# Value transforms that read strided columns of the loaded v, and query casts moved between the Sinkhorn steps

## The chip, the core and the metric

The kernel runs on one core of a Trainium2 chip. The core has a matrix engine (TensorE, PE in the profile; its weight loads are listed as PEld), a vector engine (VectorE, DVE), a scalar engine (ScalarE, ACT), a general engine (GpSimd, POOL) and a queue that only issues transfers (SyncE, SP). Engines run their own instruction streams in order and wait for one another through semaphores. The metric is the device time of one execution in microseconds; lower is better.

## The reference, cut to what matters

The inputs are q, k and v of 4 batches x 8 heads x 768 tokens x 64 (f32), a matrix sort_net of 8 x 8 for every batch and head, and the weights of a two-layer network.

```
P = sort_net                                   # [4, 8, 8, 8]
for _ in range(5):
    P = exp(P - max(P, -1)); P /= sum(P, -1) + 1e-9; P /= sum(P, -2) + 1e-9
k_sorted = einsum('bhij,bhjcd->bhicd', P, k_blocks)   # 8 blocks of 96 tokens
v_sorted = einsum('bhij,bhjcd->bhicd', P, v_blocks)
attn     = softmax(q_blocks @ k_sorted^T / 8)         # inside each block
x        = attn @ v_sorted, laid out as [3072, 512]
out      = (s * relu(x @ w_in)^2 + b) @ w_out         # [3072,512] -> 2048 -> 512
```

So each of the 8 blocks of k and v is first replaced by a mix of the 8 blocks, with the weights P that the five Sinkhorn rounds give; then follow attention inside each block and a large feed-forward network.

## The kernel before, in words

**The mix as a matmul.** A batch of k or v is loaded as a tile of 128 partitions: 8 heads x 8 blocks x 2 halves of a block. A partition holds 48 tokens (c) x 64 features (d). One column of that tile, as TensorE weights against a block-diagonal matrix built from P (`PD[b]`, in `build_pd`, L199), gives the mixed values. For k (and, with a fixed selection matrix `qid`, for q) `qk_piece` (L227) takes the 64 features of one token c as weights, `src[:, c0 + c, :]`, which lie side by side. For v, `v_piece` (L244) needs the 48 tokens of one feature d as weights, padded with zeros to 64 (`GAP`). In the loaded tile these lie 64 elements apart. The kernel before therefore makes a permuted copy `VP` (d outer, c inner), and `v_piece` reads `VP[b % 2][:, d0 + d, :]`, 64 neighbouring elements. A piece is 16 features x 2 halves, so 32 matmuls with 64 columns of weights and 64 moving columns, and one evacuation from PSUM by ScalarE ("A") or VectorE ("D"). Four pieces make a batch of v, three a batch of k or q.

**Where the copy of v comes from.** For batch 0, v is loaded as f32 by SP's queue in four parts (`v0f`, L75 to L79), and ScalarE casts and permutes a part (`permute`, L152) after each of the exps 2 to 5 of the Sinkhorn loop (L176 to L195). For batches 1 to 3, a POOL-issued load casts v to bf16 into `rawv` (`load`, L83), and POOL itself permutes it in eight copies (`v_sort`, L449, called at L453 and L514).

**The order at the start.** The program is written out by hand; each engine executes in the order of the text. PE first runs 30 matmuls on zeros (`warm`, L146 and L175), then the three query pieces, the matmul in `build_pd(0)`, 3 more on zeros, and then v, v, k, k, k, v, v (L409 to L419), and then scores (`s_piece`), attention times values (`p_piece`) and transposes (`t_piece`) of batch 0. PSUM tiles with the tag "a" have three buffers, so a piece waits until the piece three before it has been evacuated. The first two query pieces are evacuated by ScalarE after the Sinkhorn loop, the third by VectorE after the block weights. POOL issues the loads of q and k in three parts each, makes the identity, `qid` and `emat`, and then issues the loads of w_in and w_out (`load_w`); eight such loads may be under way, the next waits for the oldest.

**The steady part.** For each batch `ffn1` (L348) and `ffn2` (L376) run over two halves of the tokens; the pieces of the next batch are set between the matmul groups of `ffn2` (`halves`, L487): k at slot 0, v pieces 0 to 2 at slot 8, the fourth v piece in the second half.

Of the kernel before, what the change touches and what calls it, by code (L numbers as in the profile page):

```python
# [9 lines left out]
FP = mybir.dt.float32  # L10
BF = mybir.dt.bfloat16
AF = mybir.ActivationFunctionType
ALU = mybir.AluOpType
AX = mybir.AxisListType


def spread(t, dims):

    return bass.AP(tensor=t.tensor, offset=t.offset, ap=[list(t.ap[0])] + dims)
# [3 lines left out]
def kernel(  # L23
# [12 lines left out]
    nc = tc.nc  # L36

    B, H, S, D = q.shape
    NB = sort_net.shape[-1]
    BLK = S // NB  # L40
    BH = B * H
# [6 lines left out]
    C2 = BLK // 2  # L48
    GAP = 64
# [3 lines left out]
    CK = 16  # L53
# [3 lines left out]
    raw = [t.rearrange("b h (j z c) d -> b (h j z) (c d)", j=NB, z=2) for t in (q, k, v)]  # L57

    const = ctx.enter_context(tc.tile_pool(name="const", bufs=1))
    rawp = ctx.enter_context(tc.tile_pool(name="rawp", bufs=2))  # L60
# [5 lines left out]
    gtp = ctx.enter_context(tc.tile_pool(name="gtp", bufs=2))  # L66
# [5 lines left out]

    sn = const.tile([BH, NB, NB], FP)
    nc.sync.dma_start(out=sn, in_=sort_net.rearrange("b h i j -> (b h) i j"))
    v0f = gtp.tile([128, C2, D], FP, tag="gt", name="v0f")  # L75
    CV = C2 // 4
    for c in range(0, C2, CV):
        nc.sync.dma_start(out=v0f[:, c:c + CV, :].rearrange("p c d -> p (c d)"),  # L78
                          in_=raw[2][0][:, c * D:(c + CV) * D])  # L79

    RAW = {}

    def load(t, b, parts=1):  # L83
        ti = rawp.tile([128, C2, D], BF, tag=f"raw{t}", name=f"raw{t}")
        RAW[t, b] = ti
        n = C2 // parts
        for c in range(0, C2, n):
            nc.gpsimd.dma_start(out=ti[:, c:c + n, :].rearrange("p c d -> p (c d)"),
                                in_=raw["qkv".index(t)][b][:, c * D:(c + n) * D])
# [11 lines left out]

    zeros = const.tile([128, 512], BF)
    nc.vector.memset(zeros, 0.0)  # L103
    VP = [const.tile([128, D, GAP], BF, name=f"vp{i}") for i in range(2)]
    KS = [const.tile([128, NG, 2, GAP], BF, name=f"ks{i}") for i in range(2)]
    VS = [const.tile([KR, 2 * NG, VW], BF, name=f"vs{i}") for i in range(2)]
    nc.vector.memset(VP[0][:, :, C2:GAP], 0.0)
    nc.vector.memset(KS[0][:, :, :, C2:GAP], 0.0)
    eps = const.tile([BH, NB], FP)
    nc.vector.memset(eps, 1e-9)  # L110

    load("q", 0, 3)
    load("k", 0, 3)


    ident = const.tile([128, 128], BF)
# [12 lines left out]
    def load_w():  # L129
        wiv = moe_w_in.rearrange("(a p) f -> p a f", p=128)  # L130
        for c in range(2):
            cs = slice(c * (d_ff // 2), (c + 1) * (d_ff // 2))
            for a in range(NHP):
                nc.gpsimd.dma_start(out=wi[:, a, cs], in_=wiv[:, a, cs])
        fill_vs(0)
        wov = moe_w_out.rearrange("(f p) n -> p f n", p=128)
        for c in range(4):
            fs = slice(c * (NF // 4), (c + 1) * (NF // 4))
            nc.gpsimd.dma_start(out=wo[:, fs, :], in_=wov[:, fs, :])
# [9 lines left out]
            nc.tensor.matmul(out=z, lhsT=zeros[:, 0:128], rhs=zeros, start=True, stop=True)  # L149


    def permute(eng, b, src, cs=slice(0, C2), ds=slice(0, D)):  # L152
        o = VP[b % 2][:, ds, cs]
        i = src[:, cs, ds].rearrange("p c d -> p d c")
        if eng is nc.scalar:
            eng.copy(out=o, in_=i)  # L156
        else:
            eng.tensor_copy(out=o, in_=i)  # L158


    rstat = const.tile([BH, NB], FP)
    rrec = const.tile([BH, NB], FP)
    jsel = const.tile([128, NB], FP)
# [9 lines left out]
    nc.vector.tensor_tensor(out=sn, in0=sn, in1=rstat.broadcast_to([BH, NB, NB]),  # L173
                            op=ALU.subtract)
    warm(30)  # L175
    for it in range(5):  # L176
        nc.scalar.activation(out=sn, in_=sn, func=AF.Exp)
        if it >= 1:
            permute(nc.scalar, 0, v0f, slice((it - 1) * CV, it * CV))
        if it == 2:  # L180
            load_w()
        if it in (1, 2):
            idle[it - 1]()
        nc.vector.tensor_reduce(out=rstat, in_=sn, axis=AX.X, op=ALU.add)
        nc.vector.reciprocal(out=rrec, in_=rstat)
        nc.vector.tensor_tensor(out=sn, in0=sn, in1=rrec.broadcast_to([BH, NB, NB]), op=ALU.mult)
        if it == 4:
            break
        nc.vector.tensor_reduce(out=rstat, in_=sn.rearrange("p i j -> p j i"),
                                axis=AX.X, op=ALU.add)  # L190
        if it == 0:
            nc.vector.tensor_tensor(out=rstat, in0=rstat, in1=eps, op=ALU.add)
        nc.vector.reciprocal(out=rrec, in_=rstat)
        nc.vector.tensor_tensor(out=sn, in0=sn, in1=spread(rrec, [[0, NB], list(rrec.ap[1])]),
                                op=ALU.mult)  # L195

    PD = {}

    def build_pd(b):  # L199
        pe = psb.tile([128, 512], FP, tag="b", name="pe")  # L200
        nc.tensor.matmul(out=pe[:, 0:NB * NB], lhsT=emat[:, b, :],
                         rhs=sn.rearrange("p i j -> p (i j)"), start=True, stop=True)
        tmp = rtp.tile([128, NB, NB], FP, tag="tmp", name="tmp")
        nc.vector.tensor_tensor(out=tmp, in0=pe[:, 0:NB * NB].rearrange("p (i j) -> p i j", j=NB),
                                in1=spread(jsel, [[0, NB], list(jsel.ap[1])]), op=ALU.mult)
        pt = rtp.tile([128, NB], FP, tag="pt", name="pt")
        nc.vector.tensor_reduce(out=pt, in_=tmp, axis=AX.X, op=ALU.add)
        cs = rtp.tile([128, 1], FP, tag="cs", name="cs")
        nc.vector.tensor_reduce(out=cs, in_=pt, axis=AX.X, op=ALU.add)
        rc = rtp.tile([128, 1], FP, tag="rc", name="rc")  # L210
        nc.vector.reciprocal(out=rc, in_=cs)
        pd = const.tile([128, 2, 2, NG], BF, name=f"pd{b}")
        nc.vector.scalar_tensor_tensor(
            out=pd.rearrange("p e z (a i) -> p (e z a) i", i=NB),
            in0=spread(bm, [list(bm.ap[1]), [0, NB]]), scalar=rc,
            in1=spread(pt, [[0, 4 * NHP], list(pt.ap[1])]), op0=ALU.mult, op1=ALU.mult)
        PD[b] = pd
# [9 lines left out]
    def qk_piece(t, b, c0, eng, first=None):  # L227
        if t == "q" and c0 == 0:
            QT[b] = trp.tile([128, NG, 2, C2], BF, tag="qt", name="qt")
        src = RAW[t, b]  # L230
        mov = qid.rearrange("p e z a j -> p e z (a j)") if t == "q" else PD[b]
        dst = QT[b] if t == "q" else KS[b % 2]
        ps = psa.tile([128, CK, 2, NG], FP, tag="a", name="tp")
        for c in range(CK):
            for e in range(2):
                nc.tensor.matmul(out=ps[e * 64:(e + 1) * 64, c].rearrange("p z g -> p (z g)"),  # L236
                                 lhsT=src[:, c0 + c, :],
                                 rhs=mov[:, e].rearrange("p z g -> p (z g)"),
                                 start=True, stop=True)
        if first is not None:  # L240
            first()
        evac(eng, dst[:, :, :, c0:c0 + CK], ps.rearrange("p c z g -> p g z c"))

    def v_piece(b, d0, eng):  # L244
        ps = psa.tile([128, CK, 2 * NG], FP, tag="a", name="tv")
        for d in range(CK):
            for z in range(2):
                nc.tensor.matmul(out=ps[z * GAP:(z + 1) * GAP, d, :],  # L248
                                 lhsT=VP[b % 2][:, d0 + d, :], rhs=PD[b][:, :, z, :],
                                 start=True, stop=True)  # L250
        evac(eng, VS[b % 2][:, :, d0:d0 + CK], ps[0:KR].rearrange("p d g -> p g d"))

# [153 lines left out]
        nc.sync.dma_start(out=out[r0:r0 + 128, ns], in_=ot[:, ns])  # L406


    qk_piece("q", 0, 0, "A")  # L409
    qk_piece("q", 0, CK, "A")  # L410
    qk_piece("q", 0, 2 * CK, "D", first=lambda: build_pd(0))
    warm(3)
    v_piece(0, 0, "A")
    v_piece(0, CK, "D")
    qk_piece("k", 0, 0, "A")
    qk_piece("k", 0, CK, "D")
    qk_piece("k", 0, 2 * CK, "A")
    v_piece(0, 2 * CK, "D")
    v_piece(0, 3 * CK, "A")  # L419
    s_piece(0, 0, 0)  # L420
# [17 lines left out]
    b_bc = const.tile([128, 1], FP)  # L438
    ones = const.tile([128, 32], BF)
    nc.gpsimd.memset(ones, 1.0)  # L440
    nc.gpsimd.memset(VP[1][:, :, C2:GAP], 0.0)
    nc.gpsimd.memset(KS[1][:, :, :, C2:GAP], 0.0)
    fill_vs(1)
    for t in "vkq":
# [1 line left out]
    for t, src in ((s_bc, moe_s), (b_bc, moe_b)):  # L446
        nc.gpsimd.dma_start(out=t, in_=src.to_broadcast([128, 1]))

    def v_sort(b):  # L449
        for i in range(8):  # L450
            permute(nc.gpsimd, b, RAW["v", b], ds=slice(i * 8, (i + 1) * 8))

    v_sort(1)  # L453
    for t in "kv":
        load(t, 2)
    load_q_rows(2)
# [53 lines left out]
    for b in range(1, B):  # L510
        n = b + 1
        s0, s1 = {}, {}
        if n < B:
            v_sort(n)  # L514
            q_dma(n)
            s0, s1 = halves(n)
        ffn1(2 * b, {})
        ffn1(2 * b + 1, {})
        ffn2(2 * b, s0)
        ffn2(2 * b + 1, s1)  # L520
# [30 lines left out]
```

## Time and profile before

| what | value |
|---|---|
| runs | 236.65 and 238.05 us, median 237.35 us |
| profiled execution, span of the core | 236.1 us (the page gives no other time of it) |
| mean granted TensorE clock | 0.978 |
| TensorE busy | 221.3 us, 94% |
| weight loads (PEld) | 130.8 us, 55% |
| VectorE / ScalarE / GpSimd busy | 122.9 / 98.2 / 55.4 us |
| value transforms, L248 | 512 matmuls |
| GpSimd copies of v, L158 | 24, mean 907 ns, together 20.3 us |
| ScalarE casts of v, L156 | 4, median 1,521 ns |
| data moved by DMA | 25.03 MB, mean 106 GB/s |

The span is from the first to the last instruction of the core. Busy time is the union of an engine's instructions; matmuls are pipelined, so a matmul's listed length is its latency, and the distance from start to start is what it costs in a stream. "Issue" in the chain of waits is time in which an engine waited for nothing that the profile shows. The line of the granted clock has one digit for each of 40 slices of the span, in tenths.

### The profile page before, as it was taken

To read this page: it belongs to the slowest core of one execution; us is meant where nothing else is said; L and a number is where in the kernel's file an instruction comes from. 1 tells how busy PE (TensorE), PEld (TensorE's weight loads), DVE (VectorE), ACT (ScalarE), POOL (GpSimd) and SP (SyncE) were. 2 spreads that over 40 slices of the span, in tenths; PEclk is the share of its full clock that TensorE was granted. 3 is DMA by queue.
4 is the path that set the end of the run, shared out by engine and by line. 5 is a ranking of instruction groups with operands and counts; after the bars stand their busy time and mean duration, and the time that the engine had idled before them with its cause. 6 is when DMAs were issued, how large, how long until landed. Compare 5 with 4: busy or idle time off the path is not lost.

```text
span 236.1 us, 5888 instructions
## 1 busy us (share of the span) xinstructions
PE 221.3 (94%) x2584; PEld 130.8 (55%) x2607; DVE 122.9 (52%) x236; ACT 98.2 (42%) x123; POOL 55.4 (23%) x89
## 2 busy tenths in 40 slices
PE   7874898999998999999999999999999999999994
PEld 3553565655564655565555656656455656554453
DVE  6663426669755476444644764446355754342221
ACT  4783538554311524565212335665015255660000
POOL 7547500993663992000000000000000000000000
PEclk9998579999999999999999999999999999999999
DMA  6999999949999934920021187400112352001122
GB/s 144 286 210 193 206 209 218 190 74 205 137 190 203 170 67 124 147 37 0 3 89 50 44 114 160 86 3 3 44 47 88 64 119 45 0 1 47 52 81 90
DMA packets 37674, 25.03 MB, mean 106 GB/s; under 512 B 29200, under 2 KB 31504, under 8 KB 37648
## 3 DMA queue, kind: packets, MB, share of 16 engines
q0 software_dynamic: 17744, 12.85, 36.7%
q1 hardware_dynamic: 19904, 11.81, 20.3%
q8 instruction: 20, 0.33, 0.6%
q14 instruction: 6, 0.05, 0.1%
HBM read 27.27 MB, written 6.29 MB: 142 GB/s over the span
## 4 chain that ended last, share of the span: by engine, by line
PE 84%; DMA 4%; ACT 4%; issue 4%; DVE 2%; SPq 1%; DVEq 0%
PE hps L361 34%; PE ops L382 34%; DMA v0f<-in_v_dram 4%; PE tv L248 4%; PE tp L236 3%; PE pv L298 3%; PE sc L263 3%; PE ops L395 1%; ACT rt L371 1%; DVE x L304 1%; ACT qt L221 1%; PE z L149 1%; ACT vp L156 1%; PE tr L318 1%; SPq L78 1%
## 5 line engine op out<-in xcount | busy, mean ns | idle before, releaser
L361 PE MATMUL hps<-xt,wi 128*128 128x384 bf16 x512 | 86.3, 327 | 0.7 <-DVE x L304 0.5
L382 PE MATMUL ops<-wo,gt 128*128 128x512 bf16 x347 | 81.5, 379 | 2.2 <-issue 1.6
L371 ACT ACTIVATE rt<-hps 128x768 bf16<-128x768 f32 x64 | 51.7, 812 | 42.7 <-PE hps L361 41.1
L361 PEld LDWEIGHTS <-wi 128*128 128x128 bf16 x512 | 49.2, 98 | 32.9 <-issue 0.9
L372 DVE TENSOR_TENSOR gt<-rt 128x768 bf16<-128x768 bf16 x64 | 36.5, 572 | 44.4 <-ACT rt L371 44.2
L382 PEld LDWEIGHTS <-gt 128*128 128x128 bf16 x368 | 33.7, 98 | 37.0
L403 DVE SCALAR_TENSOR_TENSOR ot<-ops,s_bc,bias 128x512 f32<-128x512 f32 (+1 forms) x25 | 18.2, 729 | 37.2 <-PE ops L382 33.7
L268 ACT ACTIVATE at<-sc 112x768 bf16<-112x768 f32 x30 | 22.6, 809 | 32.7 <-PE sc L263 32.7
L158 POOL COPY vp<-rawv 128x384 bf16<-128x384 bf16 x24 | 20.3, 907 | 10.6 <-DMA rawv<-in_v_dram 10.6
L304 DVE TENSOR_TENSOR x<-pv,rec 96x512 bf16<-96x512 f32 x32 | 22.0, 687 | 1.1
L298 PEld LDWEIGHTS <-at 112*128 112x128 bf16 (+1 forms) x256 | 13.6, 106 | 7.2 <-ACT at L268 1.0
L223 DVE CAST vs<-tv 112x1024 bf16<-112x1024 f32 x11 | 13.3, 1223 | 6.6 <-PE tv L248 6.6
L99 POOL DMA_DIRECT2D qtok<-in_q_dram x16 | 12.4, 781 | 11.7 <-DMA rawv<-in_v_dram 6.7
L248 PE MATMUL tv<-pd,vp 128*64 128x64 bf16 x512 | 10.4, 197 | 5.0 <-issue 4.0
L221 ACT CAST vs<-tv 112x1024 bf16<-112x1024 f32 x5 | 5.1, 1021 | 22.9 <-PE tv L248 22.9
L298 PE MATMUL pv<-vs,at 112*128 112x66 bf16 (+1 forms) x256 | 14.6, 202 | 0.0
L248 PEld LDWEIGHTS <-vp 128*64 128x64 bf16 x512 | 9.2, 113 | 8.3 <-issue 7.3
L149 PE MATMUL z<-zeros 128*128 128x512 bf16 x37 | 11.9, 463 | 1.9 <-DVE zeros L103 1.2
L303 DVE RECIPROCAL rec<-pv 96x8 f32<-96x8 f32 x32 | 6.4, 200 | 13.9 <-PE pv L298 13.9
L263 PE MATMUL sc<-qt,ks 64*128 64x96 bf16 x240 | 9.0, 218 | 0.4 <-ACT vs L221 0.4
L223 DVE CAST ks<-tp 128x1024 bf16<-128x1024 f32 x7 | 8.3, 1218 | 0.2
L149 PEld LDWEIGHTS <-zeros 128*128 128x128 bf16 x39 | 4.0, 111 | 6.8 <-issue 2.8
(69 smaller groups left out, 107.9 us busy)
## 6 DMA issues: line engine op xcount, KB each, us to landing
out_dram<-ot SPq DMA_DIRECT2D x23, 256.0 KB, 2.0
rawv<-in_v_dram POOLq DMA_DIRECT2D x3, 768.0 KB, 11.9
rawk<-in_k_dram POOLq DMA_DIRECT2D x3, 768.0 KB, 7.9
wi<-in_moe_w_in_dram POOLq DMA_DIRECT2D x8, 256.0 KB, 11.8
wo<-in_moe_w_out_dram POOLq DMA_DIRECT2D x4, 512.0 KB, 14.2
v0f<-in_v_dram SPq DMA_DIRECT2D x4, 384.0 KB, 6.8
qtok<-in_q_dram POOLq DMA_DIRECT2D x16, 96.0 KB, 10.0
rawq<-in_q_dram POOLq DMA_DIRECT2D x3, 256.0 KB, 7.1
```

The lines of the kernel that those rows point to most:

```text
L149: nc.tensor.matmul(out=z, lhsT=zeros[:, 0:128], rhs=zeros, start=True, stop=True)
L158: eng.tensor_copy(out=o, in_=i)
L223: nc.vector.tensor_copy(out=out, in_=in_)
L248: nc.tensor.matmul(out=ps[z * GAP:(z + 1) * GAP, d, :], lhsT=VP[b % 2][:, d0 + d, :], rhs=PD[b][:, :, z, :], start=True, stop=True)
L268: nc.scalar.activation(out=at, in_=sc[0:KR, :, 0:TG], func=AF.Exp, scale=scale)
L298: nc.tensor.matmul(out=pv[0:m, e, n * VW:(n + 1) * VW], lhsT=atf[:, c0:c0 + m], rhs=VS[b % 2][:, e * NG + g0 + n, :], start=True, stop=True)
L304: nc.vector.tensor_tensor(out=x[:, :, hp * 128:(hp + 1) * 128].rearrange("p n (e d) -> p e n d", e=2), in0=pvv[:, :, :, 0:D], in1=rec.unsq ...
L361: nc.tensor.matmul(out=H1[i][:, f, 0:TG], lhsT=wi[:, hp, fc:fc + 128], rhs=xt[:, :, hp, :], start=(hp == 0), stop=(hp == NHP - 1))
L371: nc.scalar.activation(out=rt, in_=h, func=AF.Relu)
L372: nc.vector.tensor_tensor(out=gt[:, 2 * i:2 * i + 2, :], in0=rt, in1=rt, op=ALU.mult)
L382: nc.tensor.matmul(out=ops, lhsT=gt[:, f, m * 128:(m + 1) * 128], rhs=wo[:, f, :], start=(f == 0), stop=(f == NF - 1))
L403: nc.vector.scalar_tensor_tensor(out=ot[:, ns], in0=ops, scalar=s_bc, in1=BIAS[0][:, ns], op0=ALU.mult, op1=ALU.add)
```

## The change

The permuted copies go. `v_piece` takes the 64 weights straight from the loaded tile, `RAW["v", b][:, :, d0 + d]`, with a step of 64 elements (128 bytes). For that the loaded v is a tile of 64 instead of 48 tokens, with the last 16 set to zero, and there are three such tiles (`RV`) instead of two `rawv` and two `VP`. The f32 load of v for batch 0 on SP's queue is replaced by two casting loads on POOL's queue, behind those of q and k. In the Sinkhorn loop, which moves behind the definitions of the helpers, ScalarE evacuates a query piece after each of the exps 3, 4 and 5 instead of a part of v after 2 to 5; all three query pieces are now ScalarE's. Behind the loop the order of pieces is k, k, k, v, v, v, v, and which engine evacuates a v piece is swapped. The number of TensorE instructions is the same.

```diff
-    v0f = gtp.tile([128, C2, D], FP, tag="gt", name="v0f")
-    CV = C2 // 4
-    for c in range(0, C2, CV):
-        nc.sync.dma_start(out=v0f[:, c:c + CV, :].rearrange("p c d -> p (c d)"),
-                          in_=raw[2][0][:, c * D:(c + CV) * D])
...
     def load(t, b, parts=1):
-        ti = rawp.tile([128, C2, D], BF, tag=f"raw{t}", name=f"raw{t}")
+        if t == "v":
+            ti = RV[b % 3]
+        else:
+            ti = rawp.tile([128, C2, D], BF, tag=f"raw{t}", name=f"raw{t}")
...
-    VP = [const.tile([128, D, GAP], BF, name=f"vp{i}") for i in range(2)]
+    RV = [const.tile([128, GAP, D], BF, name=f"rv{i}") for i in range(3)]
...
-    nc.vector.memset(VP[0][:, :, C2:GAP], 0.0)
+    nc.vector.memset(RV[0][:, C2:GAP, :], 0.0)
...
     load("q", 0, 3)
     load("k", 0, 3)
+    load("v", 0, 2)
...
     for it in range(5):
         nc.scalar.activation(out=sn, in_=sn, func=AF.Exp)
-        if it >= 1:
-            permute(nc.scalar, 0, v0f, slice((it - 1) * CV, it * CV))
+        if it >= 2:
+            qk_piece("q", 0, (it - 2) * CK, "A")
         if it == 2:
             load_w()
...
-                                 lhsT=VP[b % 2][:, d0 + d, :], rhs=PD[b][:, :, z, :],
+                                 lhsT=RAW["v", b][:, :, d0 + d], rhs=PD[b][:, :, z, :],
...
-    qk_piece("q", 0, 0, "A")
-    qk_piece("q", 0, CK, "A")
-    qk_piece("q", 0, 2 * CK, "D", first=lambda: build_pd(0))
+    build_pd(0)
     warm(3)
-    v_piece(0, 0, "A")
-    v_piece(0, CK, "D")
     qk_piece("k", 0, 0, "A")
     qk_piece("k", 0, CK, "D")
     qk_piece("k", 0, 2 * CK, "A")
+    v_piece(0, 0, "D")
+    v_piece(0, CK, "A")
     v_piece(0, 2 * CK, "D")
     v_piece(0, 3 * CK, "A")
...
-    nc.gpsimd.memset(VP[1][:, :, C2:GAP], 0.0)
+    for i in (1, 2):
+        nc.gpsimd.memset(RV[i][:, C2:GAP, :], 0.0)
...
-    def v_sort(b):
-        for i in range(8):
-            permute(nc.gpsimd, b, RAW["v", b], ds=slice(i * 8, (i + 1) * 8))
-
-    v_sort(1)
...
-            v_sort(n)
             q_dma(n)
```

## The prediction

> **What bounds the kernel now.** I read the page first, then the chain of waits in order of time, then the timeline of the first 33 us and of one later stage, then the weight loads by shape. Page: engine shares, and TensorE clock in 40 slices of 5.9 us.
>
> ```profile
> PE 221.3 (94%) x2584; PEld 130.8 (55%) x2607; DVE 122.9 (52%) x236; ACT 98.2 (42%) x123; POOL 55.4 (23%) x89
> ...
> PEclk9998579999999999999999999999999999999999
> ```
>
> TensorE (PE) is busy 94% of the span; GpSimd (POOL), where the copies of v for batches 1 to 3 run, 23%. So after the start only what lengthens or shortens PE's own stream counts. The clock falls to half in slice 5: the start is the only loose part. The chain of waits there (start us, length us, what):
>
> ```profile
> 2.61 9.50 DMA v0f<-in_v_dram
> 12.11 0.02 issue
> 12.13 1.50 ACT vp L156
> 13.63 1.83 ACT qt L221 x2
> 15.46 0.04 issue
> 15.51 0.71 PE tv L248 x32
> ...
> 18.21 1.04 PE tv L248 x59
> 19.25 3.04 issue
> 22.29 0.34 PE tv L248 x5
> 22.63 0.02 issue
> 22.66 1.03 ACT vs L221
> ```
>
> The f32 load of v, its last cast and the query casts end last until 15.5; then comes a hole of 3.04 us in the middle of a value transform, in which PE waits for nothing that the profile shows. The trace's DMA packets name it: queue 8 ("instruction", 20 packets of 16,384 B for 5,204 PE rows, so 256 rows each) has a packet at 19.93 to 20.82; PE had executed 705 rows and went on at 22.29. The hole at 71.99 (0.93 us) is alike: a packet at 70.58 to 71.62, PE at row 1,980, on at 72.92. 705 and 1,980 differ by five times 256. So PE runs dry at fixed row numbers, 448 + 256k. In slow stretches the packets start some 130 to 200 rows after a multiple of 256; with the time to start I put the second request at about row 384, which PE executed at 15.95. From there to 22.29 are 6.3 us while the data DMAs are saturated.
>
> Timeline: the PE stream ahead of the queries, ScalarE's fourth exp, the end of the block weights, and a later value transform:
>
> ```profile
> 1.20 8.47 PE L149 MATMUL z<-zeros 128*128 128x512 bf16 x30 [1.20 <-DVE zeros L103]
> 9.03 0.25 ACT L177 ACTIVATE sn<-sn 32x64 f32<-32x64 f32 x1
> 9.61 1.20 PE L236 MATMUL tp<-qid,rawq 128*64 128x64 bf16 x64
> 13.74 0.35 DVE L213 SCALAR_TENSOR_TENSOR pd<-bm,rc,pt 128x128 bf16<-128x128 f32 x1
> 121.49 1.71 PE L248 MATMUL tv<-pd,vp 128*64 128x64 bf16 x96
> ```
>
> **Part 1: strided weights.** The count of value matmuls stays 512, 128 a batch. In the steady part they run in pairs (two column halves side by side): the instructions' starts repeat every 31.6 ns a pair, which is 1.6 us for the 96 matmuls above. No TensorE row of before steps over more than one element in its weights, so the price is bounded. Weight loads by shape in 112 to 191 us (mean ns after the bar's busy time), and the two DVE sums of the same 64 f32, along rows (L184) and with a step of 32 B (L189):
>
> ```profile
> L361 PEld LDWEIGHTS <-wi 128*128 128x128 bf16 x128 | 12.4, 98 | 8.2
> ...
> L248 PEld LDWEIGHTS <-vp 128*64 128x64 bf16 x256 | 4.4, 113 | 1.7 <-issue 1.7
> ```
>
> ```profile
> L184 DVE TENSOR_REDUCE rstat<-sn x5: 197/207/207, 3.2 to 11.6; 32x8 f32<-32x64 f32 x5
> ```
>
> ```profile
> L189 DVE TENSOR_REDUCE rstat<-sn x4: 253/260/261, 3.9 to 10.0; 32x8 f32<-32x64 f32 x4
> ```
>
> - From below: nothing, if 64 far columns load as fast as near ones or the load hides within the pair. A gain is excluded: the same columns are read.
> - From above: the step costs DVE (260-207)/64 = 0.83 ns an element; ScalarE's cast of v0f (step 256 B) takes 1,521 ns against 811 for 768 elements of L371, 0.92 each. 64 columns at 0.92 ns are 59 ns a load, 118 a pair if the two halves can't load side by side: 192 later pairs x 118 = 22.7 us; side by side 11.3 us.
> - Taken: DVE's ratio, the row nearest to a PE column read (a bare read from SBUF, one element a line). The 8-element sum L209 took 160 ns, so a near element costs (207-160)/56 = 0.84 ns and a far one twice that. Loads of 96 columns took 123 ns (L298, 112x96), of 64 columns 113: 0.31 ns a column, some 20 ns for 64; the pair period of 31.6 caps it. I take 24 ns more a pair: 192 x 24 ns = 4.6 us, all on PE, which has no slack there. The 0.93 us hole of batch 1 is in such a burst, and slower rows give the fetch its time: 3.7 us remain. In batch 0 the transforms lie ahead of the instruction hole, which hides 64 x 24 ns = 1.5 us; without it they would cost that too.
>
> The Trainium skill, "SBUF — State Buffer" (Specifications), speaks against this change: lines have 16 bytes, and full bandwidth wants at least two hits in each; with the new step of 128 B each column is alone on its line. It states no price; a halved rate would make the sum that of my taken value, and before shows no PE row to confirm it.
>
> **Part 2: the copies go.** POOL loses 24 x 0.86 us, at 41 to 89 us. No PE wait names them, so that is worth nothing. POOL is freed earlier to issue the loads of batch 2 (they stood behind the 10.6 us wait for rawv); first use is after 91 us. POOL gains one memset of 0.97 us before the loads of batch 1, which PE needs after 59 us: nothing.
>
> **Part 3: loads at the start.** 1.5 MB of f32 on SP's queue go; two cast loads follow k in POOL's queue. q has the DMA engines to itself, but PE's 30 warm-up matmuls end at 9.67, so that is worth nothing. q, k and v are the same 4.5 MB read that all landed by 16.6 (POOL's last wait for rawk ended at 16.59); v is first needed at about 17.9. Two more issues of 0.55 us stand ahead of the identity on POOL: DVE's jsel sum, which waited for it until 5.25, is 1.1 us later, and so the third exp is at about 8.3. All eight load slots are taken, so the first w_in load waits for q; its last landed at 27.76, the stage that needs the second half comes at about 41: hidden.
>
> **Part 4: query casts between the exps.** ScalarE keeps order, so exp 4 stands behind query cast 1, which waits for PE's matmuls behind the warm-up. PE starts them at 9.61, an evacuation follows 0.74 later (as at 121.49 and 122.23), and takes 1.01: done at 11.36, and exp 4 starts at 11.4, not at 9.03. Query cast 2 runs until 12.7; DVE's six steps take 1.45 (9.31 to 10.76), exp 5 starts 0.17 later, at 13.3 (before: 11.28, there held by the v cast). Query cast 3 runs beside DVE. From exp 5 to the end of the block weights are 2.81 (11.28 to 14.09): 16.1, so **2.0 us later**. What comes back: the three query casts are done, and PE need not wait for them (14.1 to 14.6, 0.5).
> From 16.15 on the order is k, k, k, v, v, v, v, on two evacuating engines at 1.0 and 1.2 us: the last value piece would be evacuated at about 21.9, where before had 23.68. But row 384, two pieces after the block weights in both orders, comes at 16.15 + 1.1 = 17.25, not 15.95. With the same 6.3 us the hole ends at 23.6, and what follows is as before: **1.3 us later**. If that latency were gone, the start would gain 1.8 instead.
>
> The skill's "Runtime: NRT & Kernel Launch" (Instruction fetch mechanics) has the blocks of 256 instructions, and calls the crossing mostly hidden. The 3.04 us hole contradicts it; by the rule the start would gain 1.8 us, and the measurement decides.
>
> **Sum.** 236.1 span + 1.3 (start) + 3.7 (weights) = 241.1. The runs' median of 237.35 is 1.25 above the profiled span, which is the only time the page has of it; with it **242.4 us**.
>
> **Rivals.**
> A. The far columns load for nothing: only the start remains, 237.35 + 1.3 = 238.6, not slower by what can be told. It decides if the load stays under the 31.6 ns period. For: loads have 98 to 113 ns latency that is hidden now. Against: DVE and ScalarE both pay.
> B. Columns pay the absolute 0.92 ns: 11.3 us side by side, 22.7 after one another. Value pieces of 16 pairs then take 1.4 to 2.4 us, and the start ends at 16 + 1.9 + 4 x 1.4 to 2.4, up to 3.5 later than now: 249 to 263. For: both engines show nearly the same ns. Against: PE now takes a column in 0.31 ns, so its reading is not theirs.
> C. The start gains: the fetch is served sooner, the hole closes (-1.8), and the clock holds. PE's pieces on the chain from 23.7 to 32.1, at half clock, sum to 4.4 us; full clock saves 2.2. With A's weights 233.4. Against: data DMAs are saturated there (nines up to slice 7).
>
> The clock gate works either way: the idle PE at 11.4 to 14.4 may close it earlier (k and v pieces slower, up to 1.3), or the hole may miss it (-2.2).
>
> **Chances.** Forecast (239.5 to 244.5) 0.36, A 0.30, B 0.27, C 0.07. The range, 236.5 to 254, leaves out most of C and the upper half of B. A measurement of this kernel tells about 2% from no change. Faster by that: 0.03, the far end of C. Within: A, the rest of C and under half of the forecast, 0.44. Slower: 0.53.
>
> **What would show it.** In the profile after: 96 value matmuls at 115 us and later take over 2.5 us (A: 1.7; B: 6 or more); exp 4 at about 11.4, block weights done at about 16.1; PE's hole near row 705 ends at about 23.6, none or a short one at 72; POOL without copies. I am wrong if the price of the far columns is not near a doubling, or if the fetch's 6.3 us changes with the new order of DMAs.

## The result and the profile after

The kernel after took 261.0 us (260.43 to 261.56) where the kernel before had 237.35: the ratio is 1.1015, with a 95% interval of 1.0892 to 1.1139. It is 23.65 us slower. The forecast was 242.4, and the range ended at 254. The span of the profiled execution grew from 236.1 to 259.8 us.

The page of the kernel after, engine shares and the granted clock in 40 slices:

```profile
PE 249.4 (96%) x2607; PEld 153.2 (59%) x2607; DVE 121.6 (47%) x235; ACT 93.3 (36%) x120; POOL 37.2 (14%) x68
...
PEclk9979999999997999999967999999968999999999
```

GpSimd lost its copies (55.4 to 37.2 us), VectorE and ScalarE lost work as well, and TensorE (PE) gained 28 us. Besides the dip at the start, which before had too, the clock now dips three times later on. The chain of waits of the kernel after shows where (start us, length us, what); L217 are the value matmuls, L351 the second layer:

```profile
16.50 2.77 PE tp L205 x96
19.27 7.74 PE tv L217 x128
27.03 1.03 ACT vs L190
...
129.46 5.85 PE tv L217 x96
135.31 5.46 PE ops L351 x16
140.77 1.93 PE tv L217 x32
```

The same three pieces of the same batch in the chain of the kernel before:

```profile
121.56 1.64 PE tv L248 x96
123.36 3.40 PE ops L382 x15
126.76 0.62 PE tv L248 x32
```

96 value matmuls take 5.85 us instead of 1.64, and the 16 second-layer matmuls behind them 5.46 instead of some 3.5. The windows view of the kernel after gives the reason for the second:

```profile
core 0: us, PE busy (x) PEld busy (x) DVE busy (x) ACT busy (x) POOL busy (x), PEclk, DMA share, GB/s
129.40:135.30 5.90, 5.90 (x98) 5.84 (x98) 1.23 (x1) 1.02 (x1) 0.00 (x0) 0.74 0.13 47
135.30:140.80 5.50, 5.50 (x19) 2.00 (x18) 1.98 (x2) 0.00 (x0) 0.00 (x0) 0.65 0.00 0
```

The granted clock falls while the value matmuls run and stays low behind them (column PEclk): it is full until 132.3 us, half from there to 139.1, and full again. The weight loads by shape, in 130 to 210 us (mean ns after the bar's busy time):

```profile
L217 PEld LDWEIGHTS <-rv 128*64 128x64 bf16 x248 | 14.8, 211 | 1.3 <-issue 1.3
```

211 ns instead of 113. The two loads of a pair start 5 ns apart, and most pairs follow each other after 110 ns, some after 130, instead of 31.6.

The difference of the two spans, 23.7 us, adds up from the two traces:

| part | before | after | difference |
|---|---|---|---|
| value matmuls of batches 1 to 3, with the 0.93 us hole of before | 7.9 | 23.6 | 15.7 |
| 16 second-layer matmuls behind each of the three bursts | 3 x 3.56 | 16.3 | 5.6 |
| start, up to the first matmul of the first layer | 31.84 | 34.00 | 2.2 |
| sum | | | 23.5 |

At the start, the timeline of the kernel after has the fourth exp, and the end of the block weights, where the forecast had them (11.4 and 16.1):

```profile
11.79 0.25 ACT L379 ACTIVATE sn<-sn 32x64 f32<-32x64 f32 x1
...
16.00 0.35 DVE L182 SCALAR_TENSOR_TENSOR pd<-bm,rc,pt 128x128 bf16<-128x128 f32 x1
```

### The profile page after: what moved, and what is told of

Read it like the earlier page. It is cut to its first block, busy times and chain, and to the rows that moved or that the text cites. A ratio compares the mean times of both kernels' runs of the same rounds, so it can differ in the third digit from the quotient of the medians.

```text
span 259.8 us, 5875 instructions
## 1 busy us (share of the span) xinstructions
PE 249.4 (96%) x2607; PEld 153.2 (59%) x2607; DVE 121.6 (47%) x235; ACT 93.3 (36%) x120; POOL 37.2 (14%) x68
## 3 DMA queue, kind: packets, MB, share of 16 engines
HBM read 27.27 MB, written 6.29 MB: 129 GB/s over the span
## 4 chain that ended last, share of the span: by engine, by line
PE 93%; DVE 3%; ACT 2%; issue 1%
PE ops L351 34%; PE hps L330 31%; PE tv L217 12%; PE z L148 4%; PE tp L205 4%; PE pv L267 3%; PE sc L232 3%; PE ops L364 1%; DVE x L273 1%; ACT rt L340 1%; PE tr L287 1%; PE pe L170 1%; ACT vs L190 0%; ACT qt L190 0%; PE cps L450 0%
## 5 line engine op out<-in xcount | busy, mean ns | idle before, releaser
L351 PE MATMUL ops<-wo,gt 128*128 128x512 bf16 x368 | 91.0, 398 | 0.0
L351 PEld LDWEIGHTS <-gt 128*128 128x128 bf16 x368 | 35.2, 102 | 41.2 <-issue 7.3
L237 ACT ACTIVATE at<-sc 112x768 bf16<-112x768 f32 x30 | 22.5, 809 | 45.9 <-PE sc L232 45.9
L217 PEld LDWEIGHTS <-rv 128*64 128x64 bf16 x512 | 31.2, 215 | 2.5 <-issue 2.5
L217 PE MATMUL tv<-pd,rv 128*64 128x64 bf16 x512 | 32.0, 288 | 0.0
L267 PEld LDWEIGHTS <-at 112*128 112x128 bf16 (+1 forms) x256 | 12.7, 101 | 7.5 <-ACT at L237 1.2
L267 PE MATMUL pv<-vs,at 112*128 112x66 bf16 (+1 forms) x256 | 13.8, 195 | 0.3 <-ACT at L237 0.3
L272 DVE RECIPROCAL rec<-pv 96x8 f32<-96x8 f32 x32 | 6.4, 200 | 10.2 <-PE pv L267 10.2
L205 PEld LDWEIGHTS <-rawk 128*64 128x64 bf16 x384 | 7.5, 124 | 2.2 <-issue 1.8
L232 PE MATMUL sc<-qt,ks 64*128 64x96 bf16 x240 | 8.1, 204 | 0.7 <-ACT vs L190 0.7
L205 PE MATMUL tp<-pd,rawk 128*64 128x64 bf16 x384 | 7.9, 208 | 0.5 <-DVE pd L182 0.5
```

Of the source, the lines that this page charges most:

```text
L217: nc.tensor.matmul(out=ps[z * GAP:(z + 1) * GAP, d, :], lhsT=RAW["v", b][:, :, d0 + d], rhs=PD[b][:, :, z, :], start=True, stop=True)
L237: nc.scalar.activation(out=at, in_=sc[0:KR, :, 0:TG], func=AF.Exp, scale=scale)
L267: nc.tensor.matmul(out=pv[0:m, e, n * VW:(n + 1) * VW], lhsT=atf[:, c0:c0 + m], rhs=VS[b % 2][:, e * NG + g0 + n, :], start=True, stop=True)
L351: nc.tensor.matmul(out=ops, lhsT=gt[:, f, m * 128:(m + 1) * 128], rhs=wo[:, f, :], start=(f == 0), stop=(f == NF - 1))
```

## Experiments

### The step alone, and everything but the step

e1: the kernel after, with neighbouring elements as weights.

```diff
-lhsT=RAW["v", b][:, :, d0 + d]
+lhsT=spread(RAW["v", b].rearrange("p c d -> p (c d)")[:, (d0 + d) * 48:(d0 + d) * 48 + 1], [[1, GAP]])
```

> The kernel after, with the 64 weights of a value matmul taken from 64 neighbouring elements of the same tile instead of 64 elements apart. It leaves out the right choice of columns, so its values are not the reference's; instructions, loads, order and sizes are those of the kernel after. Theory 'far columns': the step is what costs. Value matmuls go back to 31.6 ns a pair and weight loads to 113 ns, the clock stays full behind the value bursts, and only the start's part of the change is left: by the prediction's own step 1.3 us over 237.35, so 238 to 239.5, with PE's hole near row 705 back and ending at about 23.6. Rival 'order and loads': the loss comes from the new loads, the order k before v, or the clock; then it stays above 250.

Measured: 238.44 us against 237.54 of before beside it, ratio 1.0029 (0.9985 to 1.0073). Loads and the start's hole, from the groups by shape (112 to 191 us) and the chain of e1:

```profile
L217 PEld LDWEIGHTS <-rv 128*64 128x64 bf16 x256 | 4.4, 113 | 1.7 <-issue 1.7
```

```profile
22.39 2.28 issue
24.67 0.34 PE tv L217 x5
```

So all but some 0.9 us of the loss is the step. The rest of the change costs about what the start step said (1.3), within an interval that reaches from -0.4 to +1.7 us, so it can't be told from nothing. The hole is back at PE row 705 and ends at 24.67; I had said 23.6.

e2: the kernel before with its own start, and far columns in batches 1 to 3 only.

```diff
+RV = [const.tile([128, GAP, D], BF, name=f"rv{i}") for i in range(2)]
...
-lhsT=VP[b % 2][:, d0 + d, :]
+lhsT=VP[0][:, d0 + d, :] if b == 0 else RAW["v", b][:, :, d0 + d]
...
-v_sort(1)  ...  v_sort(n)
...
-s0, s1 = halves(1, [(5, LD("k", 3)), (6, LD("v", 3)), (7, lambda: load_q_rows(3))])
+s0, s1 = halves(1, [(5, LD("k", 3)), (9, LD("v", 3)), (7, lambda: load_q_rows(3))])
```

With two tiles only, v of batch 3 is loaded over batch 1 before the fourth value piece of batch 1, so 16 of the 64 features of that batch are not the reference's, and PE waits 1.1 us for that load.

> The kernel before with its own start (v of batch 0 as f32, cast and permuted by ScalarE), but batches 1 to 3 read far columns and have no copies on GpSimd. Theory 'far columns', by the comparison of the two traces: 15.9 us for the value matmuls of the three batches and 5.6 us for the matmuls behind them that run at half clock: 237.35 + 21.5 = 258.9. If most of the loss sits in the start (rival), it is under 250. If the half clock has another cause than the value bursts, 253.

Measured: 260.04 us, ratio 1.0928 (1.0816 to 1.1041). 22.5 us over before, 1.1 of them that wait: 21.4, as the two traces had it (21.5). e1's 0.9 and this 21.4 make 22.3 of the 23.65 us. What is left, batch 0's own far columns among it, lies within the interval of e2 (2.7 us to either side). The chain of e2 has the same two parts as after:

```profile
130.02 5.89 PE tv L252 x96
135.91 5.25 PE ops L386 x16
```

### How the price grows with the step

e3 to e6: the weights of e1 with a step of 2, 4, 8 and 63 elements.

```diff
-[[1, GAP]]
+[[2, GAP]]     # e4: 4, e5: 8, e6: 63, based at d0 + d
```

> The kernel after with a step of 2 elements (4 bytes) between the 64 weights, other columns than the right ones (values not the reference's). S1, 'each column pays when it lies alone on a stretch of memory': nearly no price, loads 113 ns, time near that of the near columns, 238 to 240. S2, 'any step but one element pays': loads 205 to 215 ns, pairs 110 ns, 255 to 261.

> The same with a step of 4 elements (8 bytes). S1: nothing or a part of the price, loads between 113 and 160 ns, time 238 to 248. S2: the full price, 255 to 261. The Trainium skill, 'SBUF — State Buffer' (Specifications), asks for two hits in a line of 16 bytes; by it this step would still be free.

> The same with a step of 8 elements (16 bytes). S1: the full price is reached, loads 205 to 215 ns, 255 to 261, as with 64 elements. S3, 'steps that are powers of two meet in the same part of memory, the larger the worse': a price between those of 4 and 64 elements, 242 to 252.

> The same with a step of 63 elements (126 bytes), nearly the step of the kernel after but no power of two. S1 and S2: as with 64 elements, 255 to 262, loads 205 to 215 ns. S3: nearly free, 238 to 242, and a row of 65 instead of 64 elements would then repair the kernel.

The weight loads of e3, e4, e5 and e6, from the view of the line (ns: least, median, most):

```profile
L217 PEld LDWEIGHTS <-rv x512: 107/113/117, 17.8 to 178.4; 128*64 128x64 bf16 x171
```

```profile
L217 PEld LDWEIGHTS <-rv x512: 134/157/160, 18.1 to 180.6; 128*64 128x64 bf16 x171
```

```profile
L217 PEld LDWEIGHTS <-rv x512: 192/214/217, 18.0 to 198.5; 128*64 128x64 bf16 x171
```

```profile
L217 PEld LDWEIGHTS <-rv x512: 187/208/220, 18.4 to 193.9; 128*64 128x64 bf16 x171
```

| step, elements (bytes) | stretches of 16 B that 64 columns touch | load, ns | pair, ns | time, us |
|---|---|---|---|---|
| 1 (2) | 8 | 113 | 32 | 238.44 |
| 2 (4) | 16 | 113 | 32 | 239.75 |
| 4 (8) | 32 | 157 | 60 | 241.99 |
| 8 (16) | 64 | 214 | 118 | 259.94 |
| 63 (126) | 64 | 209 | 115 | 255.33 |
| 64 (128), the kernel after | 64 | 203 | 110 | 261.0 |

The load and pair columns are medians from the traces, after 100 us; a pair's time is from start to start. The price is full from 16 bytes on and does not change between 16 and 128 bytes; a step that is no power of two doesn't help. S1 stands, S2 and S3 fall. From 32 to 64 stretches a pair goes from 60 to 110 or 118 ns: 1.6 to 1.8 ns for each stretch of 16 bytes of one load. The two loads of a pair overlap in time (5 ns apart, 203 ns each); whether they are read at once or by turns the runs don't tell. Up to 16 stretches the load hides in the pair's 32 ns. The runs of e3 to e6 are single, and their times carry the clock as well: step 63 is 5.7 us faster than 64 with almost the same pair, and its clock (40 slices) dips once behind the start and not three times:

```profile
PEclk9979999999999999999988999999999999999999
```

The Trainium skill, "SBUF — State Buffer" (Specifications), has the 16-byte line, and the runs agree on where the price stops growing. By its "need ≥2 hits per line for full bandwidth" step 4, with two columns in each line, would still be free, and that does not hold for these loads: a pair takes 60 ns instead of 32.

### The clock behind the bursts

e7: the kernel after with its first three value pieces in three slots.

```diff
-8: [V(n, 0, "D"), V(n, 1, "A"), V(n, 2, "D")]
+7: [V(n, 0, "D")], 8: [V(n, 1, "A")], 9: [V(n, 2, "D")]
```

> The kernel after with the value pieces 0, 1 and 2 of batches 1 to 3 in three slots of the second layer (7, 8, 9) instead of all in slot 8: bursts of 1.8 us with four 512-column matmuls between them instead of one of 5.8 us. Theory 'the long burst of slow pairs looks idle and closes the clock gate': the half clock behind the bursts goes and about 5.6 of 261 us come back, 255.4; the pairs keep 110 ns. Rival: the gate closes all the same, since the sum of slow work is the same: 260 to 262.

Measured: 257.32 us (257.07 to 257.57). The windows view of e7 for the three bursts of batch 2 and the stretches between (PEclk is the third column from the right):

```profile
127.60:129.60 2.00, 2.00 (x34) 1.96 (x34) 0.75 (x1) 0.00 (x0) 0.00 (x0) 1.00 0.16 59
129.60:130.50 0.90, 0.90 (x6) 0.24 (x5) 0.89 (x1) 0.00 (x0) 0.00 (x0) 1.00 0.47 171
130.50:132.50 2.00, 2.00 (x34) 1.96 (x34) 0.33 (x1) 0.00 (x1) 0.00 (x0) 1.00 0.01 3
```

The clock stays at 1.00, with the same far loads, and so it does in the other two batches. So far loads alone didn't lower it; it took the long unbroken burst. Such a burst is not always enough: in the traces of the kernel after, e2 and e5 each of the nine bursts of 5.8 to 6.0 us lowered the clock, in e6 only one of three bursts of 5.6 us. What decides there is open. 3.7 of the 5.6 us came back in the time, 4.0 in the span. Of the rest, 0.6 us lie in the value pieces (24.2 us in the three batches, 23.6 in after) and 0.4 in a later start of the first layer; the last 0.6 are open.

### Hiding the far load, which failed

e8: behind each 512-column matmul of the second layer one pair of value matmuls.

```diff
 nc.tensor.matmul(out=ops, lhsT=gt[:, f, ...], rhs=wo[:, f, :], ...)
+next(pairs[m], None)      # two value matmuls of one feature, far columns
```

> The kernel after (far columns), but in batches 1 to 3 the pairs of value matmuls no longer stand in one burst: one pair stands behind each 512-column matmul of the second layer (two behind each of eight of them), and the first attention-times-values piece of a batch moves one slot later. Theory 'a far load costs 110 ns only where nothing covers it': a 512-column matmul streams for 216 ns, the load of the next pair runs beneath it, and the pair costs near its 31.6 ns again; no burst closes the clock. The steady part comes back to that of before (15.9 + 5.6 less the few doubled pairs, 1.9), the start keeps its 2.2: 240 to 243. Rival 'PE waits out a far load wherever it stands', or the load slows the moving columns as well: pairs keep some 80 ns over before and only the clock's part comes back, 254 to 257.

Measured: 294.45 us, ratio 1.2386 (1.2311 to 1.246): far outside both. The timeline of e8, where a 512-column matmul and one pair repeat every 571 ns (median of 137 such rounds):

```profile
140.24 0.39 PE L364 MATMUL ops<-wo,gt 128*128 128x512 bf16 x1
140.56 0.32 PE L350 MATMUL tv<-pd,rv 128*64 128x64 bf16 x2
140.81 0.39 PE L364 MATMUL ops<-wo,gt 128*128 128x512 bf16 x1
```

e11: the same with the near columns of e1.

> The kernel with pairs of value matmuls between the 512-column matmuls, which took 294.45 us, with the 64 weights taken from neighbouring elements (other columns than the right ones, values not the reference's). It tells what of its 33 us over the kernel after belongs to the far load and what to the change between 128-column and 64-column weights. Theory 'every change of weight shape drains the array': a 512-column matmul and one pair took 572 ns there against 216 + 32 in bursts; with near columns, whose loads are some 90 ns shorter, some 470 to 490 remain, and the time is 270 to 280. Rival 'a far load can't run beneath a matmul and that is all': with near columns a matmul and a pair take 250 to 300 ns, and the time is 238 to 246.

Measured: 277.34 us, ratio 1.1658 (1.1581 to 1.1735). The timeline of e11, first a round with two pairs, then with one:

```profile
130.56 0.39 PE L365 MATMUL ops<-wo,gt 128*128 128x512 bf16 x1
130.88 0.25 PE L350 MATMUL tv<-pd,rv 128*64 128x64 bf16 x4
131.07 0.39 PE L365 MATMUL ops<-wo,gt 128*128 128x512 bf16 x1
...
134.56 0.39 PE L365 MATMUL ops<-wo,gt 128*128 128x512 bf16 x1
134.88 0.22 PE L350 MATMUL tv<-pd,rv 128*64 128x64 bf16 x2
135.03 0.39 PE L365 MATMUL ops<-wo,gt 128*128 128x512 bf16 x1
```

A round with one near pair takes 472 ns, against 216 + 32 in bursts, and a round with two takes 503: a second pair costs the 31 ns of a burst. So going to and fro costs some 224 ns a round whatever the columns, 36 us for the 161 rounds, and time and round are where the first theory of e11 had them. The far load adds 99 ns to a round with one pair, more than the 78 that it costs in a burst: nothing of it is hidden. So some two thirds of e8's loss against e1 are the going to and fro. That the change of weight shape is its cause, and a drain of the array, is argued, not shown: the pair also has other moving columns and another PSUM tile. Whether a far load hides behind long matmuls with weights of its own shape is left open.

### The instruction hole

e9: the kernel before with 180 more instruction rows ahead of the queries.

```diff
-nc.tensor.matmul(out=z, lhsT=zeros[:, 0:128], rhs=zeros, ...)
+for i in range(4): nc.tensor.matmul(out=z[:, i*128:(i+1)*128], lhsT=zeros[:, 0:128], rhs=zeros[:, 0:128], ...)
```

> The kernel before, with each of its 30 warm-up matmuls on zeros of 512 columns split into four of 128: the same work on PE, 180 more instruction rows ahead of the queries. Theory 'instruction fetch': PE runs dry at rows 448 + 256k, and the request goes out some 320 rows earlier. The rows move these points 180 rows forward in the program: the one that gave the 3.04 us hole in the last value piece now lies in the k pieces, its request goes out in the query pieces at about 11.5 and is served by 17.8, when PE gets there; the next lies in the scores. The hole shrinks below 1 us, the last value piece is evacuated some 1.8 us sooner, and the clock stays full from 22 to 32 (another 2): 233 to 236. Rival: the hole belongs to the value piece (a wait that the profile does not show): same place, 3 us, 237.35.

Measured: 238.69 us, ratio 1.002 (0.9975 to 1.0066). The chain of e9:

```profile
17.29 0.19 PE tp L239
17.48 2.79 issue
20.27 0.67 PE tp L239 x31
...
23.94 0.27 PE sc L266 x7
24.21 2.52 issue
26.74 0.24 PE sc L266
```

The hole left the value piece and sits in a k piece, and a second one stands in the scores: at rows 705 and 961, as in 448 + 256k. That it follows row numbers is shown. That moving it forward would shrink it is wrong. In e9 the instruction packets start at 11.30, 17.98, 24.34 and 30.43, in before at 13.90, 19.93 and 26.22: one block of 256 rows every 6 to 6.7 us, and the next seems to be asked for only when the last has come. More rows only use up the supply sooner.

e10: fewer rows ahead, 8 f32 matmuls for the 30.

```diff
+zerof = const.tile([128, 512], FP)
...
-warm(30)
+for _ in range(8): nc.tensor.matmul(out=z, lhsT=zerof[:, 0:128], rhs=zerof, ...)
```

> The kernel before with its 30 warm-up matmuls replaced by 8 in f32 of 512 columns on zeros, about the same stretch of PE work in 52 instruction rows less. Theory 'instruction fetch, one block of 256 rows per some 6.2 us while the data DMAs are saturated': the point where PE runs dry moves 52 rows back in the program, behind the last value piece and the first three score pieces. The last value piece is evacuated at about 20 to 20.5 instead of 22.66, the first attention exp starts 2 us sooner, and the dry stretch, now in front of the fourth score piece, is shorter than 2 us. 234 to 236.5. Rival: the exps gain nothing because the fourth score piece and the values pieces behind it wait for the same block: 237 to 238. If the f32 matmuls are shorter than taken, PE is idle ahead of the queries and the clock is at half in the k and v pieces: 238 to 240.

Measured: 237.57 us, ratio 0.9969 (0.9933 to 1.0006). The time is the rival's: the first blocks came later (15.34 and 22.15 us instead of 13.90 and 19.93), and the hole, now in the first score piece, was longer. The trace has two loads and two matmuls for each f32 matmul, so the rows saved were probably 28 and not 52. The chain of e10:

```profile
20.78 0.20 PE sc L267
20.98 3.56 issue
```

e12: the kernel before; half of w_in and all of w_out wait for the last value piece of batch 0.

```diff
...
+gate = const.tile([KR, 2 * NG], BF)
+nc.gpsimd.tensor_copy(out=gate, in_=VS[0][:, :, D - 1])
+load_w1()                       # w_in, second half
 for t in "vkq": load(t, 1)
+load_w2()                       # w_out
```

> The kernel before with fewer data DMAs under way at its start: the second half of w_in and all of w_out are issued on POOL only after the last value piece of batch 0 has been evacuated (a small copy on POOL waits for it). Nothing is left out. Theory 'PE's instruction blocks come late because the data DMAs fill the engines': with q, k, v and half of w_in under way only, the engines are freer from about 17 on, the block that arrives at 22.29 in before comes by 19 to 21, the hole of 3.04 us shrinks to 0 to 1.5 us, and the clock may stay open: 233 to 236.5. If w_in's second half or w_out then comes too late for the layers, some of it is lost again. Rival 'a block takes some 6 us whatever else moves': hole as before, 237 to 239.

Measured: 242.88 us, ratio 1.0197 (1.0141 to 1.0254). The second block came at 19.42 to 20.31 and the hole was 1.92 us; the third started 1.1 us after PE went on, not 3.9 as in before, at a DMA share of 0.04 (20 to 24 us) against 1.06. So a block came sooner where the data DMAs were idle, by one trace of each kernel; the second block, with part of them still under way, gained only 0.5 us. What was gained was lost waiting for w_in, the first line of the waits of PE in e12 (the releaser that it names had long been done):

```profile
PE hps L368 <- DVE x L311: 6.4, 2, 5.9
PE tv L255 <- issue: 1.9, 1, 1.9
```

e13 and e14: as e12, but waiting for the last k piece, w_out ahead of batch 1; in e14 all of w_in is issued as in before.

```diff
-nc.gpsimd.tensor_copy(out=gate, in_=VS[0][:, :, D - 1])
+nc.gpsimd.tensor_copy(out=gate, in_=KS[0][:, :, 0, C2 - 1])
```

> As the kernel with late weights of the network (242.88 us), which reached the first layer 2.7 us sooner than before (29.16 instead of 31.84) and then lost 5.9 us waiting for w_in's second half, but the copy on POOL that holds the loads back waits for the last k piece instead of the last v piece, and w_out goes ahead of the loads of batch 1. Nothing is left out. Theory 'the hole and the half clock behind it come from the data DMAs under way': the half of w_in is under way some 4 us sooner and is there when the layer asks for it, the 2.7 us stay: 234 to 236. Rival 'the loads are needed that early': any gain at the start is lost again in waits of the first layer or of the bias: 237.5 to 241.

> The same, but all of w_in is issued as in before and only w_out and batch 1 are held back until the last k piece. Nothing is left out. If the block that PE waits for is held up by what is under way at 16 to 20, that is w_in still, the hole stays as in before (3 us) and only the blocks after it come sooner: 236.5 to 238. If w_out alone made the difference, 234 to 236.

Measured: e13 236.49 us against 238.14 beside it, ratio 0.9915 (0.9875 to 0.9955), e14 237.22, ratio 0.9991 (0.9953 to 1.003). By the medians e13 is 0.7% below before, less than the 2% that count as a change here. The profile of e13 has the hole as in before:

```profile
19.10 3.15 issue
22.25 0.34 PE tv L255 x5
```

But the profiled execution is the longest of the twelve, 238.69 us, and gained nothing, so it can't say where a gain comes from. The twelve times go with the granted clock: the four at 0.978 took 238.1 to 238.7 us, as before mostly does, and the eight at 0.991 to 0.993 took 234.6 to 237.6. So the gain comes with a shorter stretch at low clock; whether the hole was shorter there too, no trace shows. e14 is no faster than before, and its hole was longer, 3.75 us.

## Why the prediction was wrong

**The step that failed is the value taken in part 1**: "I take 24 ns more a pair: 192 x 24 ns = 4.6 us". Measured are 110 - 31.6 = 78 ns a pair, 15.0 us, and 15.7 in the chains, where a pair takes 118 ns on average and the hole of before is gone. The kind of cost was right (the load, not the matmul, sets the pair's period), its price was too small by a factor of 3: by the prediction's own sign, 96 value matmuls took 5.85 us, next to B's 6 and not to the forecast's 2.5. I took VectorE's ratio of far to near elements, twofold, and applied it to 0.31 ns a column. That number is no price of a column: it compares loads of 112 x 96 and 128 x 64, and the row with 128 columns shown beside them takes 98 ns, less than 64 columns do. And near columns share a stretch of 16 bytes, so their price says nothing of a stretch's. An absolute time for each far access would have come closer: VectorE's 0.84 + 0.83 ns for a far element makes 107 ns for 64 columns, and the pair takes 110. This match was found afterwards and may be luck; 0.83 to 0.92 ns for each of a pair's 128 columns, one after another, makes 106 to 118 as well.

**The clock was missed in the steady part**, 5.6 us by the traces. I priced the clock gate only at the start (+1.3 to -2.2). That a burst of slow pairs can lower it, with PE busy 96% of the time, was in no case; e7 shows it. Of the 18.6 us between forecast and result 12.0 are the price (15.7 for 3.7), 5.6 the clock and 0.9 the start (2.2 for 1.3). With the right price alone the forecast would have been 254.4. That 261 lies inside B's 249 to 263 is partly luck: its 11.3 and 22.7 us lie to either side of the 15.7, and the clock is in neither.

**Part 2** held: the 20 us of copies on GpSimd were worth nothing (e1, without them, is not faster than before), and PE waited for no load of batch 2 or 3 in the kernel after.

**Part 3** held: PE waits for no load at the start of the kernel after, and jsel is 1.04 us later (6.29).

**Part 4** held in its steps: the fourth exp at 11.79 (11.4 forecast), the block weights done at 16.36 (16.1). Its sum, 1.3 us later, can be tested only with near columns: 0.9 us by the medians (e1), with the hole ending at 24.67 instead of 23.6. In e1's trace the block weights were done at 16.90 and the clock was at half from 17.35 to 20.76, during the k pieces, which the prediction had allowed for; so row 384 came at 18.37 instead of 17.25, and the 6.3 us from there to the hole's end held. Behind the hole the half clock was shorter than in before (6.8 us, not 10.2), which gave about 1 us back, so that the sum came near is partly luck. With far columns the value pieces of batch 0 take 7.74 us, no hole is left, and the last evacuation ends at 28.05 instead of 23.68. 2.2 of these 4.4 us come back before the first layer, where PE has its full clock and before had half.

**The hole at 72** is gone, as said: slow rows give the fetch its time.

## What to carry to other kernels

Before weights are taken from a layout as it lies, count the 16-byte stretches that a load touches: up to 16 were free here, beyond 32 each cost about 1.7 ns of TensorE, and the copies on an idle engine cost nothing. When no row shows an operation, put the absolute time of the access on another engine beside the ratio; here the absolute time was nearer. And price a slow burst on TensorE twice, once for itself and once for the clock behind it, which fell in 10 of 12 bursts of 5.6 to 6.0 us; bursts of 2 us between dense matmuls kept the clock here.

## What the runs showed of the hardware

- 64 bf16 columns of weights load in 113 ns up to a step of 4 bytes, 157 at 8, and 203 to 214 from 16 to 128 bytes; the loads of the two column halves overlap in time.
- PE can be busy all the time and still be granted half its clock (132.3 to 139.1 us of the kernel after).
- A 512-column matmul and a pair of 64-column matmuls by turns take 472 ns a round with near columns (e11) and 571 with far ones (e8); in bursts they take 216 + 32.
- PE's instructions come in blocks of 256 rows, 6 to 6.7 us apart while data DMAs fill the engines (before, e9); 3 us of before's start are such a hole, which more rows (e9) or fewer (e10) only moved. The Trainium skill, "Runtime: NRT & Kernel Launch" (Instruction fetch mechanics), has the blocks, but calls the crossing mostly hidden; here it cost 3.04 us.
